# Attention backward on one core: where the X column fills of a row pair stand among its eight units

## The chip, the cores and the metric

One core of one Trainium2 chip runs the whole program. The metric is the device time of one launch in microseconds (us), taken as the median of several runs. Where two kernels are compared, the ratio is the mean time of one kernel's fast runs over that of the other's fast runs of the same rounds, so it isn't quite the ratio of the medians that I quote beside it.

The engines carry their short names: PE multiplies matrices (PEld is its weight load), ACT evaluates functions, DVE and POOL work elementwise, SP issues transfers.

## The reference, cut to what matters

The kernel computes a block of an attention network and all its gradients, for 2 sequences of 4000 tokens and 144 channels.

```python
def _fwd_reference(x, w_qkv, w_att_out, ...):
    xa = _layernorm(x, axis=-1)
    qkv = jnp.einsum('btd,de->bte', xa, w_qkv)
    ...
    scores = jnp.einsum('btd,bsd->bts', q, k) * D ** (-0.5)
    p = _softmax(scores, axis=-1)
    attn = jnp.einsum('bts,bsd->btd', p, v)
    ...                                   # a local branch with convolutions, a merge
def reference(x, ..., grad_out):
    _out, _vjp = jax.vjp(_f, x, ...)
    return (_out, *_vjp(grad_out))
```

## The kernel before

The tokens of a sequence are cut into 32 blocks of 128. The attention stage walks over the 32 row blocks, here called rows `i`. Each row has four *units*, one for every quarter of the columns. Two rows make a *pair* of eight units. I number a pair's units 0 to 7, and units 0 and 4 begin a row.

A unit computes scores `pS` and their gradient counterpart `pD` for 1000 columns, in two halves. A tile `pS`, `pD` or `X` takes one *bank*, a buffer for PE's results; each of the three has two banks. ACT turns `pS` into exponentials `P` (named Pm in the profile), and DVE turns `pD` and `P` into `Sm`:

```python
def unit(i, c2):
    ...
    pS = [ps_s.tile([128, 512], F32, tag="S") for h in range(2)]   # two banks in all
    pD = [ps_d.tile([128, 512], F32, tag="D") for h in range(2)]   # two banks in all
    for r, o_ in enumerate((pS[0], pD[0], pS[1], pD[1])):           # the 16 odd channels, L1768
        nc.tensor.matmul(o_[:, 0:SC], QBr[rr, bi, :], S.XR[rr, c2, 0:SC], start=True, stop=False)
    for w_, p_ in ((QTm, pS), (BTm, pD)):                           # the 128 others, L1772
        for h in range(2):
            nc.tensor.matmul(p_[h][:, 0:SC], w_[:, bi, :], S.xaT[...], start=False, stop=True)
    with tc.high_priority():
        for h in range(2):
            nc.scalar.activation(P[:, pb, c1:c1 + SC], pS[h], ACT.Exp, accum_out=...)
            nc.vector.scalar_tensor_tensor(Sm[:, pb, c1:c1 + SC], pD[h], 1.0, P[...], ..., accum_out=...)
            if c2 == 0 and h == 0 and i > 0:
                row_end2(i - 1)
```

When a row's four units are through, its row sums exist. The *row end* then scales the row's vectors:

```python
def row_end(i):
    nc.vector.reduce_sum(ld[:], ld8[:], axis=AX.X)
    nc.vector.reciprocal(rl[:], ld[:, 0:1])
    ...                                                  # nd, nr and Qs on POOL
    nc.scalar.activation(br[:], S.B_t[:, i, :], ACT.Copy, scale=rl[:])
def row_end2(i):                                          # one unit later, after the first product
    nc.vector.scalar_tensor_tensor(Bt[:, pb, :], Qs[:, pb, :], nd[:], br[:], op0=ALU.mult, op1=ALU.add)
```

The finished row is used twice. `yz` multiplies its transposed blocks by the tokens: 16 matmuls in every unit, for the row two before. After a row's last `yz`, ACT and DVE scale the result `y` (Q_t, yd, B_t in the profile; B_t is that finished result, `Bt` the scaled vector of the newest row). The *X fills* add the row's columns to a running sum `acc`. There are eleven fills for a pair, each of three column blocks with four matmuls a block (the last has two blocks). They run during the next pair:

```python
def xfill(pr, f):
    X = ps_x.tile([128, 3, D], F32, tag="x")              # two banks in all
    for jj in range(nj):
        for kk, i in enumerate((2 * pr, 2 * pr + 1)):
            nc.tensor.matmul(X[:, jj, :], Sm[:, i % NP, ...], Qs[:, i % 4, :], start=(kk == 0), stop=False)
            nc.tensor.matmul(X[:, jj, :], P[:, i % NP, ...], Bt[:, i % 4, :], start=False, stop=(kk == 1))
    ...                                                   # acc += X, on DVE or on ACT and POOL
fills = {(1, 0): 0, (1, 1): 1, (2, 0): 2, (2, 1): 3, (3, 0): 4, (3, 1): 5,
         (4, 0): 6, (4, 1): 7, (5, 1): 8, (6, 0): 9, (6, 1): 10}        # (unit, place): fill
```

In a unit PE runs the score matmuls, then place 0 (a fill, if there is one, and a step of the local branch), the `yz` matmuls, and place 1 (a fill and a step). Units 0 and 7 hold no fill.

Of the kernel before, what the change touches and what calls it, by code (L numbers as in the profile page):

```python
# [8 lines left out]
F32 = mybir.dt.float32  # L9
# [5 lines left out]
D = 144  # L15
# [244 lines left out]
def phase_att(k, W, b, S):  # L260
# [6 lines left out]
    with ExitStack() as es:  # L267
# [149 lines left out]
        def stage_C2(i):  # L417
# [3 lines left out]
            if len(pending) == R_ or i == NB - 1:  # L421
                for j0 in range(0, NB, 3):
                    nj = min(3, NB - j0)
                    X = ps_x.tile([PB, 3, D], F32, tag="x")
                    for jj in range(nj):
                        j = j0 + jj
                        n = len(pending)
                        for kk, (bi_, bpb, bsb) in enumerate(pending):
                            nc.tensor.matmul(X[:, jj, :], Sbuf[0:PB, bsb, j * 128:j * 128 + PB], Qs[:, bpb, :], start=(kk == 0), stop=False)
                            nc.tensor.matmul(X[:, jj, :], Pbuf[0:PB, bpb, j * 128:j * 128 + PB], Bs[:, bpb, :], start=False, stop=(kk == n - 1))  # L430
                    xs = xsp.tile([PB, 3, D], F32, tag="xs")
                    nc.scalar.copy(xs[:, 0:nj, :], X[:, 0:nj, :])
                    nc.gpsimd.tensor_tensor(S.acc[:, j0:j0 + nj, :], xs[:, 0:nj, :], S.acc[:, j0:j0 + nj, :], op=ALU.add)
# [15 lines left out]
def phase_local(k, W, b, S, A):  # L449
# [6 lines left out]
    if True:  # L456
        with ExitStack() as el:
# [185 lines left out]
            def pass3(g):  # L643
# [20 lines left out]
                s1 = sm.tile([PB, GB], F32, tag="s1")  # L664
                nc.vector.reduce_sum(s1[:], dgn[:], axis=AX.X)
                prod = wk.tile([PB, GB, D], F32, tag="prod", bufs=1)
                nc.vector.tensor_tensor(prod[:], dgn[:], gn_tp[:, rsl, :], op=ALU.mult)
                s2 = sm.tile([PB, GB], F32, tag="s2")
                nc.vector.reduce_sum(s2[:], prod[:], axis=AX.X)
                nc1 = sm.tile([PB, GB], F32, tag="nc1")  # L670
# [388 lines left out]
NBK = 32  # L1059
# [659 lines left out]
def phase_attn(k, W, b, S):  # L1719
    nc, tc = k.nc, k.tc  # L1720
    NP = 3
    GW = NBK * 128
    with ExitStack() as es:
# [5 lines left out]
        ps_x = es.enter_context(tc.tile_pool(name="at_psx", bufs=2, space=PSUM))  # L1729
        ps_y = es.enter_context(tc.tile_pool(name="at_psy", bufs=1, space=PSUM))  # L1730
        ps_f = es.enter_context(tc.tile_pool(name="at_psf", bufs=1, space=PSUM))
        P = ab.tile([128, NP, GW], BF, name="Pm")
        Sm = ab.tile([128, NP, GW], BF, name="Sm")
        for t in (P, Sm):
            nc.gpsimd.memset(t[:, :, TT_:], 0.0)
        Qs = ab.tile([128, 4, D], BF, name="Qs")
        Bt = ab.tile([128, 4, D], BF, name="Bt")
        QB = ab.tile([128, 4, 128], BF, name="QB")
        nc.gpsimd.memset(QB[:], 0.0)
        st = {}  # L1740
# [3 lines left out]
        def jit(g):  # L1744
            r = slice(g * 4, g * 4 + 4)
            jt[g] = [xp.tile([128, 4, 128], BF, tag=t_, name=t_) for t_ in ("QTm", "BTm", "QBr")]
            for off, src in ((0, S.Q_t), (32, S.B_t), (64, S.Q_t), (96, S.B_t)):
                nc.gpsimd.tensor_scalar(QB[:, :, off:off + DR], src[:, r, 128:D], 1.0, 0.0, op0=ALU.mult, op1=ALU.add)
            for step in range(3):
                yield 'P', 2  # L1750
                src = (S.Q_t[:, r, 0:128], S.B_t[:, r, 0:128], QB[:])[step]
                pj = ps_f.tile([128, 4, 128], BF, tag="f", name="pj")
                for j in range(4):
                    nc.tensor.transpose(pj[:, j, :], src[:, j, :], id_[:])
                nc.scalar.copy(jt[g][step][:], pj[:])

        def unit(i, c2):
            g, bi = divmod(i, 4)
            QTm, BTm, QBr = jt[g]
            pb = i % NP  # L1760
            if c2 == 0:
                st["ld", i] = sm.tile([128, 2, 8], F32, tag="ld8", name="ld8")
            ld8 = st["ld", i]
            pS = [ps_s.tile([128, 512], F32, tag="S", name="pS") for h in range(2)]
            pD = [ps_d.tile([128, 512], F32, tag="D", name="pD") for h in range(2)]
            for r, o_ in enumerate((pS[0], pD[0], pS[1], pD[1])):
                rr = slice(32 * r, 32 * r + DR)
                nc.tensor.matmul(o_[:, 0:SC], QBr[rr, bi, :], S.XR[rr, c2, 0:SC], start=True, stop=False)  # L1768
            c0 = 2 * c2 * SC
            for w_, p_ in ((QTm, pS), (BTm, pD)):  # L1770
                for h in range(2):
                    nc.tensor.matmul(p_[h][:, 0:SC], w_[:, bi, :], S.xaT[:, c0 + h * SC:c0 + (h + 1) * SC], start=False, stop=True)  # L1772
            with tc.high_priority():
                for h in range(2):
                    c1 = c0 + h * SC
                    n = 2 * c2 + h
                    nc.scalar.activation(P[:, pb, c1:c1 + SC], pS[h][:, 0:SC], ACT.Exp, accum_out=ld8[:, 0, n:n + 1])  # L1777
                    nc.vector.scalar_tensor_tensor(Sm[:, pb, c1:c1 + SC], pD[h][:, 0:SC], 1.0, P[:, pb, c1:c1 + SC], op0=ALU.mult, op1=ALU.mult,  # L1778
                                                   accum_out=ld8[:, 1, n:n + 1])
                    if c2 == 0 and h == 0 and i > 0:  # L1780
                        row_end2(i - 1)

        def flip(key, i, h):

            t = st[key, i, h] = ab.tile([128, 16, 128], BF, tag=key, bufs=3, name=key)
            nc.sync.dma_start_transpose(out=t[:], in_=(P if key == "PT" else Sm)[:, i % NP, h * 2048:(h + 1) * 2048])
# [17 lines left out]
        def row_end2(i):  # L1804
            pb = i % 4
            nc.vector.scalar_tensor_tensor(Bt[:, pb, :], Qs[:, pb, :], st.pop(("nd", i))[:], st.pop(("br", i))[:], op0=ALU.mult, op1=ALU.add)  # L1806
# [16 lines left out]
                nc.scalar.activation(yd[:], y[:, 0, :], ACT.Copy, scale=nr[:])  # L1823
                nc.vector.scalar_tensor_tensor(S.Zn[:, i, :], y[:, 1, :], rl[:], yd[:], op0=ALU.mult, op1=ALU.add)  # L1824

        def xfill(pr, f):
            j0 = f * 3
            nj = min(3, NBK - j0)
            X = ps_x.tile([128, 3, D], F32, tag="x", name="X")
            for jj in range(nj):  # L1830
                j = j0 + jj
                for kk, i in enumerate((2 * pr, 2 * pr + 1)):
                    nc.tensor.matmul(X[:, jj, :], Sm[:, i % NP, j * 128:(j + 1) * 128], Qs[:, i % 4, :], start=(kk == 0), stop=False)  # L1833
                    nc.tensor.matmul(X[:, jj, :], P[:, i % NP, j * 128:(j + 1) * 128], Bt[:, i % 4, :], start=False, stop=(kk == 1))  # L1834
            a_ = S.acc[:, j0:j0 + nj, :]
            if f % 2 == 1:
                xs = xp.tile([128, 3, D], F32, tag="xs", name="xs")
                nc.scalar.copy(xs[:, 0:nj, :], X[:, 0:nj, :])  # L1838
                nc.gpsimd.tensor_tensor(a_, xs[:, 0:nj, :], a_, op=ALU.add)  # L1839
            else:  # L1840
                nc.vector.tensor_tensor(a_, X[:, 0:nj, :], a_, op=ALU.add)  # L1841



        fills = {(1, 0): 0, (1, 1): 1, (2, 0): 2, (2, 1): 3, (3, 0): 4, (3, 1): 5, (4, 0): 6, (4, 1): 7, (5, 1): 8, (6, 0): 9, (6, 1): 10}
        Q = Steps()
        local_steps(k, W, b, S, es, ps_f, Q)
        with tc.manual_schedule():
            for _ in jit(0):
                pass  # L1850
            for g in range(1, NGR):
                Q.add(32 * g - 16, jit(g))
            for i in range(NBK + 2):
                pr, half = i // 2 - 1, i % 2
                for c2 in range(4):
                    if i < NBK:
                        unit(i, c2)
                    if c2 == 0 and i == NBK:
                        row_end2(i - 1)
                    for place in range(2):  # L1860
                        f = fills.get((half * 4 + c2, place))
                        if f is not None and 0 <= pr < NBK // 2:
                            xfill(pr, f)
                        Q.place()
                        if place == 0 and 0 <= i - 2 < NBK:
                            yz(i - 2, c2)
                        if place == 0:
                            key, fi, h = (("PT", i - 1, 1), (None, 0, 0), ("PT", i, 0), ("ST", i, 0))[c2]
                            if key and 0 <= fi < NBK:
                                flip(key, fi, h)  # L1870
                            if c2 == 2 and 0 <= i - 1 < NBK:
                                flip("ST", i - 1, 1)
                    if c2 == 3 and i < NBK:
                        row_end(i)
            while Q.tasks:
                Q.place()
# [442 lines left out]
```

## Time and profile before

| | before |
|---|---|
| time, median of 3 runs | 1528.79 us (1527.81 to 1530.97) |
| span of the profiled run | 1533.1 us |
| attention, first unit to last, both sequences | 1039.5 us |
| one pair, mean from the fifth row on | 32.8 us at full clock (33.25 us with the parts at half clock) |

The first line of the profile page gives busy time, share of the span and instruction count for each engine.

```profile
PE 1364.5 (89%) x15366; PEld 990.8 (65%) x15366; DVE 886.1 (58%) x3021; ACT 820.7 (54%) x2473; POOL 567.4 (37%) x1049
```

PE looks nearly full, but the Trainium skill warns of this line (Perfetto Trace Analysis, "Identifying the Most-Contended Engine"): matmul busy time isn't a good measure of how close PE is to its limit, because matmuls are pipelined. The next two lines are groups of that page. Their columns are line, engine, operation, tiles, shapes and count, then busy us and mean ns of one, then idle us of the engine just before them and what ended it.

```profile
L1834 PE MATMUL X<-Bt,Pm 128*128 128x144 bf16 x2048 | 293.6, 227 | 1.0 <-DVE Bt L1806 1.0
...
L1768 PE MATMUL pD<-XR,QBr 16*128 16x500 bf16 x512 | 131.0, 392 | 21.1 <-DVE Sm L1778 19.6
```

One X matmul "takes" 227 ns. Yet in the timeline they start every 62 ns, so three or four are always in flight, and an idle engine shows as idle only after the last of them has drained. I therefore read stalls from start to start. The following lines are timelines of PE, ACT and DVE for the passage from unit 7 to unit 1 of one pair. The columns are start us, us, engine, line, operation, tiles, shapes and count, with the idle time before it and its releaser in brackets.

```profile
303.00 0.38 PE L1768 MATMUL pD<-XR,QBr 16*128 16x500 bf16 x1
...
305.29 1.16 PE L1816 MATMUL y<-xaa,PT 128*128 128x144 bf16 x16
...
306.63 0.38 PE L1768 MATMUL pD<-XR,QBr 16*128 16x500 bf16 x1
...
307.17 0.37 PE L1768 MATMUL pD<-XR,QBr 16*128 16x500 bf16 x1 [0.15 <-DVE Sm L1778]
307.47 0.60 PE L1772 MATMUL pS<-xaT,QTm 128*128 128x500 bf16 x2
...
303.18 0.38 ACT L1821 ACTIVATE Q_t<-y,rl 128x144 bf16<-128x144 f32 x1
303.44 0.39 ACT L1823 ACTIVATE yd<-y,nr 128x144 f32<-128x144 f32 x1
304.54 0.42 ACT L1801 ACTIVATE br<-B_t,rl 128x144 f32<-128x144 bf16 x1 [0.71 <-DVE rl L1794]
304.86 0.57 ACT L1777 ACTIVATE Pm<-pS 128x500 bf16<-128x500 f32 x1
...
303.86 0.37 DVE L1824 SCALAR_TENSOR_TENSOR B_t<-y,rl,yd 128x144 bf16<-128x144 f32 x1 [0.40 <-ACT yd L1823]
304.15 0.16 DVE L1792 TENSOR_REDUCE ld<-ld 128x2 f32<-128x16 f32 x1
304.34 0.16 DVE L1794 RECIPROCAL rl<-ld 128x1 f32<-128x1 f32 x1
305.55 0.68 DVE L1778 SCALAR_TENSOR_TENSOR Sm<-pD,Pm 128x500 bf16<-128x500 f32 x1 [1.05 <-ACT Pm L1777]
...
306.15 0.36 DVE L1806 SCALAR_TENSOR_TENSOR Bt<-Qs,nd,br 128x144 bf16<-128x144 bf16 x1
306.43 0.67 DVE L1778 SCALAR_TENSOR_TENSOR Sm<-pD,Pm 128x500 bf16<-128x500 f32 x1
```

Unit 0 starts at 303.00 and unit 1 at 306.63. In unit 1 the last of the four L1768 matmuls should start some 10 ns after the first; it starts 0.54 us later, because DVE's second product of unit 0 has only then left its `pD` bank. The profile calls 0.15 us of this idle.

The other lines show why the product is late. ACT scales the `y` of unit 7 (303.18 and 303.44), and DVE makes B_t of it. Only then does DVE reach the row sum and its reciprocal (304.15, 304.34). ACT's `br` waits for that reciprocal, and unit 0's exponentials stand behind `br` (304.86). The products (305.55, 306.43) and `Bt` (306.15) follow. I call this the *row-end chain*.

### The profile page before, as it was taken

How to read it: one execution, taken by the hardware profiler on the slowest of the kernel's cores; microseconds unless marked ns; L12 is line 12 of the kernel's file. 1: busy time of each engine (PE TensorE's matmuls, PEld its weight loads, DVE VectorE, ACT ScalarE, POOL GpSimd, SP SyncE). 2: the span in 40 equal slices, each digit the busy share in tenths (PEclk: the TensorE clock that was granted, in tenths of full speed). 3: DMA queues.
4: the chain of work that ended last, by engine and by line, in shares of the span. 5: the costliest groups of instructions: out<-in, count | busy, mean ns of one | idle time of the engine just before them, and what ended most of it. 6: DMA issues, size and time to landing. Idle time of an engine off the chain costs nothing. (4 is left out here: it accounts for less than half of the span.)

```text
span 1533.1 us, 40191 instructions
## 1 busy us (share of the span) xinstructions
PE 1364.5 (89%) x15366; PEld 990.8 (65%) x15366; DVE 886.1 (58%) x3021; ACT 820.7 (54%) x2473; POOL 567.4 (37%) x1049
## 2 busy tenths in 40 slices
PE   5989999999999999899779999999999999989932
PEld 3727767676776767687553767677667667868610
DVE  5545676676676666344335666676776676534332
ACT  4746656566656654343365666666656565444210
POOL 2233444444344433343232444344444442334200
PEclk9959999999999999999896999999999999999955
DMA  5348978898988799654525988998999988856320
GB/s 143 105 86 149 169 136 162 155 170 150 163 153 163 131 192 171 146 171 116 158 77 99 165 153 147 170 164 154 164 160 147 170 158 163 162 156 180 78 87 13
DMA packets 652289, 220.66 MB, mean 144 GB/s; under 512 B 589876, under 2 KB 649012, under 8 KB 652084
## 3 DMA queue, kind: packets, MB, share of 16 engines
q1 hardware_dynamic: 651220, 217.89, 73.0%
q8 instruction: 122, 2.00, 0.6%
q14 instruction: 83, 0.68, 0.2%
q10 hardware_dynamic: 864, 0.09, 0.0%
HBM read 58.00 MB, written 25.13 MB: 54 GB/s over the span
## 5 line engine op out<-in xcount | busy, mean ns | idle before, releaser
L1778 DVE SCALAR_TENSOR_TENSOR Sm<-pD,Pm 128x500 bf16<-128x500 f32 x512 | 331.2, 675 | 286.8 <-ACT Pm L1777 226.4
L1777 ACT ACTIVATE Pm<-pS 128x500 bf16<-128x500 f32 x512 | 294.9, 582 | 125.9 <-PE pS L1772 123.0
L1839 POOL TENSOR_TENSOR acc<-xs,acc 128x432 f32<-128x432 f32 x160 | 179.8, 1124 | 395.9 <-ACT xs L1838 393.9
L1834 PE MATMUL X<-Bt,Pm 128*128 128x144 bf16 x2048 | 293.6, 227 | 1.0 <-DVE Bt L1806 1.0
L1833 PE MATMUL X<-Qs,Sm 128*128 128x144 bf16 x2048 | 293.7, 227 | 0.5 <-POOL Qs L1797 0.5
L1833 PEld LDWEIGHTS <-Sm 128*128 128x128 bf16 x2048 | 201.5, 98 | 19.2 <-issue 2.6
L1834 PEld LDWEIGHTS <-Pm 128*128 128x128 bf16 x2048 | 201.2, 98 | 18.8 <-issue 2.1
L1772 PE MATMUL pS<-xaT,QTm 128*128 128x500 bf16 x512 | 162.0, 400 | 0.0
L1772 PE MATMUL pD<-xaT,BTm 128*128 128x500 bf16 x512 | 160.1, 396 | 0.0
L1838 ACT COPY xs<-X 128x432 f32<-128x432 f32 x160 | 83.2, 520 | 138.4 <-PE X L1834 137.4
L1816 PE MATMUL y<-xaa,PT 128*128 128x144 bf16 x2048 | 150.4, 227 | 1.2 <-DVE B_t L1824 1.2
L1768 PE MATMUL pD<-XR,QBr 16*128 16x500 bf16 x512 | 131.0, 392 | 21.1 <-DVE Sm L1778 19.6
L1816 PE MATMUL y<-xaa,ST 128*128 128x144 bf16 x2048 | 149.0, 226 | 0.0
L1816 PEld LDWEIGHTS <-PT 128*128 128x128 bf16 x2048 | 134.1, 98 | 9.2 <-issue 1.6
L1816 PEld LDWEIGHTS <-ST 128*128 128x128 bf16 x2048 | 131.9, 98 | 6.5
L1841 DVE TENSOR_TENSOR acc<-X,acc 128x432 f32<-128x432 f32 x192 | 111.1, 578 | 42.3 <-PE X L1834 42.3
L1768 PE MATMUL pS<-XR,QBr 16*128 16x500 bf16 x512 | 117.3, 395 | 5.4 <-ACT Pm L1777 4.1
L1777 ACT ACTIVATION_READ_ACCUMULATOR Pm<-pS 128x1 f32 x512 | 102.2, 200 | 0.0
L1772 PEld LDWEIGHTS <-QTm 128*128 128x128 bf16 x512 | 29.3, 98 | 106.6 <-issue 106.6
L1772 PEld LDWEIGHTS <-BTm 128*128 128x128 bf16 x512 | 52.4, 102 | 65.3 <-issue 11.4
L2009 POOL TENSOR_SCALAR cc<-xaa,n 128x144 f32<-128x144 bf16 x64 | 36.2, 572 | 99.3 <-DVE n L2006 84.1
L1768 PEld LDWEIGHTS <-QBr 16*128 16x128 bf16 x1024 | 30.3, 91 | 61.7 <-issue 36.7
(584 smaller groups left out, 2602.6 us busy)
## 6 DMA issues: line engine op xcount, KB each, us to landing
gs<-in_grad_out_dram SPq DMA_DIRECT2D x24, 720.0 KB
gtap<-gn_d SPq DMA_DIRECT2D x16, 720.0 KB
dh_d<-dh SPq DMA_DIRECT2D x32, 144.0 KB
dhr<-dh_d SPq DMA_DIRECT2D x16, 288.0 KB
gs<-in_grad_out_dram SPq DMA_DIRECT2D x8, 540.0 KB
xg<-in_x_dram SPq DMA_DIRECT2D x28, 144.0 KB
dug_d<-dug SPq DMA_DIRECT2D x16, 144.0 KB
gn_d<-gn_t SPq DMA_DIRECT2D x32, 72.0 KB
```

What stands on the lines that cost most here:

```text
L1768: nc.tensor.matmul(o_[:, 0:SC], QBr[rr, bi, :], S.XR[rr, c2, 0:SC], start=True, stop=False)
L1772: nc.tensor.matmul(p_[h][:, 0:SC], w_[:, bi, :], S.xaT[:, c0 + h * SC:c0 + (h + 1) * SC], start=False, stop=True)
L1777: nc.scalar.activation(P[:, pb, c1:c1 + SC], pS[h][:, 0:SC], ACT.Exp, accum_out=ld8[:, 0, n:n + 1])
L1778: nc.vector.scalar_tensor_tensor(Sm[:, pb, c1:c1 + SC], pD[h][:, 0:SC], 1.0, P[:, pb, c1:c1 + SC], op0=ALU.mult, op1=ALU.mult, accum_out=l ...
L1816: nc.tensor.matmul(y[:, w, :], src[:, jj, :], S.xaa[:, j, :], start=(j == 0), stop=(j == NBK - 1))
L1833: nc.tensor.matmul(X[:, jj, :], Sm[:, i % NP, j * 128:(j + 1) * 128], Qs[:, i % 4, :], start=(kk == 0), stop=False)
L1834: nc.tensor.matmul(X[:, jj, :], P[:, i % NP, j * 128:(j + 1) * 128], Bt[:, i % 4, :], start=False, stop=(kk == 1))
L1838: nc.scalar.copy(xs[:, 0:nj, :], X[:, 0:nj, :])
L1839: nc.gpsimd.tensor_tensor(a_, xs[:, 0:nj, :], a_, op=ALU.add)
L1841: nc.vector.tensor_tensor(a_, X[:, 0:nj, :], a_, op=ALU.add)
L2009: nc.gpsimd.tensor_scalar(cc[:, q, :], S.xaa[:, 2 * p + q, :], n[:, 1, q:q + 1], n[:, 0, q:q + 1], op0=ALU.mult, op1=ALU.add)
```

## The change

The change leaves no unit without a fill. Fills 0 and 1 are split by row. The half of the pair's first row runs in unit 7, before the pair's own turn. The half of its second row runs in unit 0. The other nine fills move along.

```diff
-        def xfill(pr, f):
+        def xfill(pr, f, rows=(0, 1)):
-            X = ps_x.tile([128, 3, D], F32, tag="x", name="X")
-            for jj in range(nj):
-                j = j0 + jj
-                for kk, i in enumerate((2 * pr, 2 * pr + 1)):
-                    nc.tensor.matmul(... Sm ... Qs ..., start=(kk == 0), stop=False)
-                    nc.tensor.matmul(... P ... Bt ..., start=False, stop=(kk == 1))
+            if 0 in rows:
+                st["X", f] = ps_x.tile([128, 3, D], F32, tag="x", name="X")
+            X = st["X", f]
+            for kk in rows:
+                i = 2 * pr + kk
+                for jj in range(nj):
+                    j = j0 + jj
+                    nc.tensor.matmul(... Sm ... Qs ..., start=(kk == 0 and jj == 0), stop=False, skip_group_check=True)
+                    nc.tensor.matmul(... P ... Bt ..., start=False, stop=(kk == 1), skip_group_check=True)
+            if 1 not in rows:
+                return
 ...
-        fills = {(1, 0): 0, (1, 1): 1, (2, 0): 2, ...}                    # as above
+        fills = {(0, 1): ((0, (1,)), (1, (1,))), (1, 0): ((2, (0, 1)),), (1, 1): ((3, (0, 1)),), (2, 1): ((4, (0, 1)),),
+                 (3, 0): ((5, (0, 1)),), (3, 1): ((6, (0, 1)),), (4, 1): ((7, (0, 1)),), (5, 0): ((8, (0, 1)),),
+                 (5, 1): ((9, (0, 1)),), (6, 1): ((10, (0, 1)),), (7, 1): ((0, (0,)), (1, (0,)))}
```

A half-finished fill holds three column blocks open in one PSUM bank, which is why the start flag now stands on the first matmul of the bank alone. The Trainium skill (PSUM — Partial Sum Buffer, "The four PSUM rules") says that a starting matmul clears the accumulation bits of the whole bank, and that groups which are open at once in a bank may have the flag on the first matmul issued there alone. The changed kernel follows that rule. Whole fills now also run row by row instead of block by block.

More of the change, by code (lines that the diff above doesn't have):

```diff
@@ L1824, in yz @@
                 nc.vector.scalar_tensor_tensor(S.Zn[:, i, :], y[:, 1, :], rl[:], yd[:], op0=ALU.mult, op1=ALU.add)
-        def xfill(pr, f):
+        def xfill(pr, f, rows=(0, 1)):
             j0 = f * 3
             nj = min(3, NBK - j0)
-            X = ps_x.tile([128, 3, D], F32, tag="x", name="X")
-            for jj in range(nj):
-                j = j0 + jj
-                for kk, i in enumerate((2 * pr, 2 * pr + 1)):
-                    nc.tensor.matmul(X[:, jj, :], Sm[:, i % NP, j * 128:(j + 1) * 128], Qs[:, i % 4, :], start=(kk == 0), stop=False)
-                    nc.tensor.matmul(X[:, jj, :], P[:, i % NP, j * 128:(j + 1) * 128], Bt[:, i % 4, :], start=False, stop=(kk == 1))
+            if 0 in rows:
[5 more added lines that the diff above has]
+                    j = j0 + jj
+                    nc.tensor.matmul(X[:, jj, :], Sm[:, i % NP, j * 128:(j + 1) * 128], Qs[:, i % 4, :], start=(kk == 0 and jj == 0), stop=False, skip_group_check=True)
+                    nc.tensor.matmul(X[:, jj, :], P[:, i % NP, j * 128:(j + 1) * 128], Bt[:, i % 4, :], start=False, stop=(kk == 1), skip_group_check=True)
+            if 1 not in rows:
+                return
+            st.pop(("X", f))
             a_ = S.acc[:, j0:j0 + nj, :]
@@ L1841, in xfill @@
                 nc.vector.tensor_tensor(a_, X[:, 0:nj, :], a_, op=ALU.add)
-        fills = {(1, 0): 0, (1, 1): 1, (2, 0): 2, (2, 1): 3, (3, 0): 4, (3, 1): 5, (4, 0): 6, (4, 1): 7, (5, 1): 8, (6, 0): 9, (6, 1): 10}
+        fills = {(0, 1): ((0, (1,)), (1, (1,))), (1, 0): ((2, (0, 1)),), (1, 1): ((3, (0, 1)),), (2, 1): ((4, (0, 1)),), (3, 0): ((5, (0, 1)),), (3, 1): ((6, (0, 1)),),
+                 (4, 1): ((7, (0, 1)),), (5, 0): ((8, (0, 1)),), (5, 1): ((9, (0, 1)),), (6, 1): ((10, (0, 1)),), (7, 1): ((0, (0,)), (1, (0,)))}
         Q = Steps()
@@ L1860, in phase_attn @@
                     for place in range(2):
-                        f = fills.get((half * 4 + c2, place))
-                        if f is not None and 0 <= pr < NBK // 2:
-                            xfill(pr, f)
+                        for f, rows in fills.get((half * 4 + c2, place), ()):
+                            q = pr + 1 if rows == (0,) else pr
+                            if 0 <= q < NBK // 2:
+                                xfill(q, f, rows)
                         Q.place()
```

## The prediction

> **What bounds the kernel.** Page, part 1: PE busy 1364.5 of 1533.1 us (89%), DVE 58%, ACT 54%. The chain that ended last is mostly PE. The attention stage (timeline, about 83 to 620 and 803 to 1340 us) is bound by PE's in-order stream. PE's busy share hides stalls there, because matmuls overlap, so I read start-to-start gaps in the timeline. TensorE: Matmul & The Clock Gate (the Trainium skill, "Back-to-back issue gap") gives N/2.4 + 2.5 ns, 62.5 ns at N=144; the timeline agrees (X and y matmuls start 62 ns apart). Per row pair (eight units) PE takes 33.1 us, of which about 29.2 us is pace (my sum) and 3.9 us stall.
>
> Where the stalls are, at full clock, ns per unit (PE work / stall at the next unit's head):
> - unit 0: 2502 / 1125, plus 500 inside
> - unit 7: 2560 / 195
> - unit 4: 3945 / 350; unit 5: 3349 / 300
> - units 1, 2, 3, 6 (work 3.8 us and over): about none.
>
> Cause: units 0 and 7 hold no X fills, so PE reaches the next unit's 16-row score matmuls before ACT's exponentials (0.58 us each) and DVE's products (0.67 us) have freed pS and pD. In unit 0 they are late because ACT and DVE first run row-end work after unit 7's y: scaled copies of y, reciprocal, br, then the exponential.
>
> **What the change does.** No arithmetic is added or removed: same 4096 X matmuls and evacuations. 12 X matmuls (0.75 us) move into each of units 0 and 7, one more fill into unit 5; units 2, 4 and 6 lose a fill each. New: fills 0 and 1 hold both X buffers from unit 7 to unit 0, and unit 0's halves need Bt of the row just ended. In the trace Bt ends 3.8 us after unit 0's start, 0.9 us after y ends. So PE will wait for Bt inside unit 0, but less: unit 7's y, where the row-end chain begins, now ends 0.75 us earlier relative to unit 0's start. I expect Bt about 3.0 us after it and a wait of 0.3 us.
>
> **Sum per pair (estimate from these lengths),** head stalls counted with the unit that caused them: units 7+0 7.4 us before, 7.3 after though 1.5 us of work moved in; unit 1 unchanged; unit 2 -0.6; unit 4 -0.25 (0.75 less work, but its row-end chain then shows as about 1 us of stall at unit 5's head); unit 5 +0.45; unit 6 -0.55. Net -1.1 us of 33.1, all on the critical path. Some 30 of 32 pairs: -33 us, discounted to -29 because waits move and ps_f (one buffer) stays. Head and tail stages do not change.
>
> **Prediction:** 1500 us, range 1481 to 1520. Faster by over 2%: 0.46; within 2%: 0.51; slower by over 2%: 0.03.
>
> **What would show it.** The stall at unit 1's head (0.96 us start to start, the pD score matmul waiting for DVE's Sm) falls under 0.3; the X<-Bt group shows a new wait for Bt in unit 0, under 0.5 us each; unit 5's head stall grows; PE busy falls by about 25 us at equal counts; DVE, ACT and POOL busy stay within 1%.
>
> **What would make it wrong.** Bt may come no earlier, if local work on ACT rather than y's end sets it: then some 16 us are saved. Unit 4's chain, with fill 6's DVE sum now ahead of the row sum, may lose more than 0.5 us. Or the even spread also removes ps_f stalls, and over 40 us are saved. The half-clock spells (3.4 us each, a few in attention) may shift either way.

## The result, and the profile after

| | before | after |
|---|---|---|
| median | 1528.93 us (4 runs) | 1510.10 us (4 runs, 1509.91 to 1512.44) |
| ratio | | 0.9871, 95% interval 0.9847 to 0.9894 |
| span of the profiled run | 1533.1 us | 1510.5 us |
| attention, first unit to last, both sequences | 1039.5 us | 1008.5 us |
| drains, last unit's start to last X matmul, both | 39.0 us | 42.5 us |
| from the first drain to the second attention stage | 179.4 us | 181.2 us |
| from the second drain to the end | 192.1 us | 195.6 us |

The change saves 18.8 us, and the ratio says 1.3%. The outputs are right. The same line of the page, and the same two groups, for the changed kernel:

```profile
PE 1351.8 (89%) x15366; PEld 991.2 (66%) x15366; DVE 875.8 (58%) x3021; ACT 815.9 (54%) x2473; POOL 566.1 (37%) x1049
```

```profile
L1837 PE MATMUL X<-Bt,Pm 128*128 128x144 bf16 x2048 | 292.2, 226 | 15.6 <-DVE Bt L1806 15.5
...
L1768 PE MATMUL pD<-XR,QBr 16*128 16x500 bf16 x512 | 121.3, 390 | 10.8 <-DVE Sm L1778 10.4
```

The idle time before the `pD` matmuls fell from 21.1 to 10.8 us, and a new wait stands before the X matmuls that need `Bt`: 15.6 us instead of 1.0. The timelines of PE, ACT and DVE for unit 0 of one pair of the changed kernel show it. DVE's lines begin with the last product of unit 7.

```profile
328.16 0.38 PE L1768 MATMUL pS<-XR,QBr 16*128 16x500 bf16 x1
...
330.34 0.23 PE L1836 MATMUL X<-Qs,Sm 128*128 128x144 bf16 x1
331.51 0.22 PE L1837 MATMUL X<-Bt,Pm 128*128 128x144 bf16 x1 [0.94 <-DVE Bt L1806]
...
332.61 0.38 PE L1768 MATMUL pS<-XR,QBr 16*128 16x500 bf16 x1
...
329.48 0.41 ACT L1801 ACTIVATE br<-B_t,rl 128x144 f32<-128x144 bf16 x1 [0.84 <-DVE rl L1794]
329.80 0.57 ACT L1777 ACTIVATE Pm<-pS 128x500 bf16<-128x500 f32 x1
...
326.47 0.67 DVE L1778 SCALAR_TENSOR_TENSOR Sm<-pD,Pm 128x500 bf16<-128x500 f32 x1
...
328.09 0.37 DVE L1824 SCALAR_TENSOR_TENSOR B_t<-y,rl,yd 128x144 bf16<-128x144 f32 x1 [0.16 <-ACT yd L1823]
328.38 0.30 DVE L1604 TENSOR_SCALAR a__5755<-a__5755 128x576 bf16<-128x576 bf16 x1
328.71 0.46 DVE L1605 TENSOR_TENSOR h_t<-a__5755,hs 128x576 bf16<-128x576 bf16 x1
329.08 0.16 DVE L1792 TENSOR_REDUCE ld<-ld 128x2 f32<-128x16 f32 x1
329.28 0.17 DVE L1794 RECIPROCAL rl<-ld 128x1 f32<-128x1 f32 x1
330.49 0.68 DVE L1778 SCALAR_TENSOR_TENSOR Sm<-pD,Pm 128x500 bf16<-128x500 f32 x1 [1.04 <-ACT Pm L1777]
...
331.09 0.36 DVE L1806 SCALAR_TENSOR_TENSOR Bt<-Qs,nd,br 128x144 bf16<-128x144 bf16 x1
331.38 0.67 DVE L1778 SCALAR_TENSOR_TENSOR Sm<-pD,Pm 128x500 bf16<-128x500 f32 x1
```

Unit 0 starts at 328.16. Its first X matmul runs at 330.34, and the second waits 1.17 us for `Bt`, which DVE finishes at 331.45. On DVE the row's last product started at 326.47, but B_t and two operations of the local branch (L1604, L1605) stand in the queue ahead of the row sum (329.08). `br` waits for the reciprocal, and the exponentials wait behind `br`. Unit 1 then starts with no stall at all (332.61): the wait for `Bt` has taken the place of the wait for the bank.

The next table gives mean lengths in us of the eight units at full clock, from the fifth row on (23 to 28 units each; a unit with any half-clock time in it is left out). A stall at a unit's head is counted with the unit before it, which causes it. The pair is taken from start to start of its units, so it can differ from the sum of the rows by 0.1 us.

| unit | before | after | difference | predicted difference |
|---|---|---|---|---|
| 7 and 0 together | 7.33 | 7.82 | +0.49 | -0.1 |
| 1 | 4.06 | 4.15 | +0.09 | 0 |
| 2 | 4.35 | 3.64 | -0.71 | -0.6 |
| 3 | 4.38 | 4.38 | 0 | 0 |
| 4 | 4.70 | 4.44 | -0.26 | -0.25 |
| 5 | 4.08 | 4.47 | +0.39 | +0.45 |
| 6 | 3.98 | 3.41 | -0.57 | -0.55 |
| pair | 32.82 | 32.23 | -0.59 | -1.1 |

With their half-clock parts the pairs took 33.25 us before and 32.23 us after, 1.02 us less: five half-clock spells (stretches of the clock record at 0.5, 3.41 us each) lie in these pairs in the trace of the kernel before, and none in that of the changed kernel.

Three mean stalls a pair matter for the argument. The one at unit 1's head went from 0.96 us to none, the one at unit 5's head from 0.33 to 0.66 us, and the wait for `Bt` inside unit 0 from none to 0.69 us.

Outside these stretches the changed kernel's profiled run lost 8.8 us: 3.5 us in the drains and 5.3 us in the stages after them, whose code is the same. The next lines give busy us (and count) of PE, PEld, DVE, ACT and POOL in the two stretches that follow the drains, then the granted PE clock, the DMA share and GB/s. First the kernel before, then the changed one:

```profile
623.60:803.10 179.50, 149.87 (x1693) 118.53 (x1690) 68.97 (x282) 76.58 (x221) 61.27 (x119) 0.92 0.47 136
1341.00:1533.10 192.10, 129.39 (x1398) 92.08 (x1395) 68.49 (x286) 50.53 (x158) 42.77 (x84) 0.80 0.37 103
```

```profile
608.30:789.50 181.20, 151.64 (x1692) 119.98 (x1689) 68.84 (x282) 76.56 (x221) 61.09 (x119) 0.91 0.46 135
1314.90:1510.50 195.60, 135.65 (x1399) 96.70 (x1396) 68.47 (x286) 50.51 (x158) 42.67 (x84) 0.76 0.36 101
```

All five engines do the same work in both. The clock differs: 0.80 against 0.76 in the last stretch. In the trace's clock record the half-clock time of the two stretches is 27.2 and 78.0 us before, 33.8 and 92.7 us after.

### The profile page after: what moved, and what is told of

It reads as the page before. It is cut to its first block, busy times and chain, and to the rows that moved or that the text cites. A ratio compares the mean times of both kernels' runs of the same rounds, so it can differ in the third digit from the quotient of the medians.

```text
span 1510.5 us, 40195 instructions
## 1 busy us (share of the span) xinstructions
PE 1351.8 (89%) x15366; PEld 991.2 (66%) x15366; DVE 875.8 (58%) x3021; ACT 815.9 (54%) x2473; POOL 566.1 (37%) x1049
## 5 line engine op out<-in xcount | busy, mean ns | idle before, releaser
L1777 ACT ACTIVATE Pm<-pS 128x500 bf16<-128x500 f32 x512 | 294.5, 581 | 89.8 <-PE pS L1772 86.8
L1837 PE MATMUL X<-Bt,Pm 128*128 128x144 bf16 x2048 | 292.2, 226 | 15.6 <-DVE Bt L1806 15.5
L1772 PE MATMUL pD<-xaT,BTm 128*128 128x500 bf16 x512 | 156.9, 389 | 0.0
L1816 PEld LDWEIGHTS <-PT 128*128 128x128 bf16 x2048 | 132.8, 98 | 11.5 <-issue 2.6
L1816 PEld LDWEIGHTS <-ST 128*128 128x128 bf16 x2048 | 132.6, 98 | 11.6
L1768 PE MATMUL pD<-XR,QBr 16*128 16x500 bf16 x512 | 121.3, 390 | 10.8 <-DVE Sm L1778 10.4
L1768 PE MATMUL pS<-XR,QBr 16*128 16x500 bf16 x512 | 111.7, 393 | 1.7 <-ACT QBr L1755 1.4
```

The costliest lines, as they stand in the source:

```text
L1772: nc.tensor.matmul(p_[h][:, 0:SC], w_[:, bi, :], S.xaT[:, c0 + h * SC:c0 + (h + 1) * SC], start=False, stop=True)
L1777: nc.scalar.activation(P[:, pb, c1:c1 + SC], pS[h][:, 0:SC], ACT.Exp, accum_out=ld8[:, 0, n:n + 1])
L1816: nc.tensor.matmul(y[:, w, :], src[:, jj, :], S.xaa[:, j, :], start=(j == 0), stop=(j == NBK - 1))
L1837: nc.tensor.matmul(X[:, jj, :], P[:, i % NP, j * 128:(j + 1) * 128], Bt[:, i % 4, :], start=False, stop=(kk == 1), skip_group_check=True)
```

## The experiments

Eleven runs beside the changed kernel's own. Runs of one heading ran on one chip and are compared with each other. The changed kernel itself wasn't run in the first call; there its 1510.10 us comes from its own run, in which the kernel before took 1528.93 us against 1529.90 us in the first call.

### First call: four runs around the row-end chain

**bt_stale.** Unit 0's halves use a row that is long ready. Its output is wrong, which doesn't matter for the time.

```diff
-   nc.tensor.matmul(X[:, jj, :], P[...], Bt[:, i % 4, :], ...)
+   nc.tensor.matmul(X[:, jj, :], P[...], Bt[:, (i - 1 if rows == (1,) else i) % 4, :], ...)
```

> Changed kernel, but unit 0's half fills multiply by the scaled row (Bt) of the row before, which is ready long ago, so that PE has no wait for Bt there; the result is wrong on purpose, the work is the same. Changed kernel: 1510.1 us, mean wait for Bt in unit 0 0.69 us per pair, head stall of unit 1 zero. Theory (one row-end chain holds both Bt and, 0.67 us later, the free pD bank): the wait moves to the pD score matmul at unit 1's head, about 0.4 us of it comes back there, and at most 0.3 us per pair is saved: 1499 to 1507 us. Rival (the split made a new wait that is pure loss): all 0.69 us per pair comes back, about 21 us: 1486 to 1492 us.

Measured: 1495.29 us, between the two ranges. The trace shows what the edit itself did. The wait for `Bt` (0.69 us) was gone, 0.29 us came back at unit 1's head, and a pair took 32.03 us instead of 32.23. The other 0.2 us came back elsewhere in units 0 to 2 and isn't traced further. The attention stages took 1003.2 us, 5.3 us less than in the changed kernel's trace. The rest of the 15 us lies in stages that the edit doesn't touch, where half-clock time was 19.7 and 80.8 us. So the theory's mechanism and its limit of 0.3 us a pair hold for the attention stage, though less came back at unit 1's head than the 0.4 us expected, and the total was blurred; stale_g80 below repeats it.

**seven_front.** Unit 7's halves stand ahead of its `yz` matmuls.

```diff
-   (7, 1): ((0, (0,)), (1, (0,)))}
+   (7, 0): ((0, (0,)), (1, (0,)))}
```

> Changed kernel, but unit 7's 12 X matmuls stand before its y matmuls rather than after them. The count of matmuls in each unit is the same. Theory (the row-end chain starts at the end of unit 7's y, and the X matmuls after y buy it 0.75 us): Bt comes later after unit 0's start, about 3.7 us instead of 3.2, the wait for Bt rises from 0.69 to about 1.2 us per pair, 1520 to 1528 us. Rival (only how many matmuls a unit holds counts, not their place): 1507 to 1513 us.

Measured: 1523.72 us. `Bt` ended 3.62 us after unit 0's start (3.22 in the changed kernel), and the wait for it was 0.91 us. Matmul counts per unit are the same, so place counts and not only number. The wait rose less than expected, by 0.22 us rather than 0.5. Unit 0 itself grew from 4.28 to 4.69 us.

**after_sum** and **before_sum.** The row sum and its reciprocal are issued straight after the row's last product, on the changed kernel and on the kernel before.

```diff
     with tc.high_priority():
         for h in range(2):
             ...                                    # exponentials and products
+        if c2 == 3:
+            row_sum(i)                             # reduce_sum and reciprocal, taken out of row_end
```

> Changed kernel, with the row sum and its reciprocal issued on DVE straight after the row's last product rather than behind the local work and the y scaling that follow. Theory (the row-end chain sets what is left): Bt 2.3 to 2.7 us after unit 0's start instead of 3.2, wait for Bt under 0.2 us instead of 0.69, head stall of unit 5 under 0.25 us instead of 0.66; 0.8 to 1.1 us per pair saved, 1476 to 1486 us. Rival (ACT and DVE throughput sets it, whatever the order): less than 5 us saved, 1505 us and over.

Measured: 1474.15 us, ratio to the kernel before 0.9638 (0.9608 to 0.9669). The wait for `Bt` fell from 0.69 to 0.26 us a pair, unit 5's head stall from 0.66 to 0.10 us, and a pair took 31.05 us, 1.18 us less. The gain and the time lie just beyond the expected ranges, and `Bt` (2.8 us after unit 0's start in the mean) and its wait just short of theirs. These timelines of PE, ACT and DVE show the same unit 0 as above, which now starts at 322.53:

```profile
322.53 0.38 PE L1768 MATMUL pS<-XR,QBr 16*128 16x500 bf16 x1
...
324.71 0.23 PE L1842 MATMUL X<-Qs,Sm 128*128 128x144 bf16 x1
325.01 0.22 PE L1843 MATMUL X<-Bt,Pm 128*128 128x144 bf16 x1
...
322.90 0.42 ACT L1807 ACTIVATE br<-B_t,rl 128x144 f32<-128x144 bf16 x1
...
320.84 0.67 DVE L1778 SCALAR_TENSOR_TENSOR Sm<-pD,Pm 128x500 bf16<-128x500 f32 x1
...
321.55 0.17 DVE L1793 TENSOR_REDUCE ld<-ld 128x2 f32<-128x16 f32 x1
321.76 0.17 DVE L1795 RECIPROCAL rl<-ld 128x1 f32<-128x1 f32 x1
...
322.61 0.36 DVE L1830 SCALAR_TENSOR_TENSOR B_t<-y,rl,yd 128x144 bf16<-128x144 f32 x1
...
324.59 0.37 DVE L1812 SCALAR_TENSOR_TENSOR Bt<-Qs,nd,br 128x144 bf16<-128x144 bf16 x1
```

The row sum now follows the product at once (321.55), `br` waits for nothing, and the first exponential starts 0.74 us after unit 0's start instead of 1.64 us. `Bt` ends 2.43 us after the start instead of 3.29 us.

> The kernel before, with the same early row sum and nothing else. Theory: what the spread hid is mostly this chain, so the early sum alone brings about as much as the change: head stall of unit 1 0.96 to about 0.3 us, of unit 5 0.33 to under 0.1, 1498 to 1510 us. Rival (units 0 and 7 are too short whatever the chain: two exponentials and two products take 2.5 us): under 8 us saved, 1521 us and over.

Measured: 1488.58 us, ratio 0.9740 (0.9704 to 0.9776). I had expected about the change's own gain, and it was twice that: the early sum alone saves 41 us where the change saves 19 us. A pair took 31.68 us. Unit 1's head stall fell only to 0.64 us, which fits the rival's point that units without fills are too short; with the spread on top (after_sum) it is gone, and the time falls by another 14 us. So over the whole pair the late sum cost more than the empty units did. The two don't act at the same place, though: of the 1.14 us that the early sum saves in a pair at full clock, 0.7 us lies in units 4 and 5 (4.70 to 4.24 us and 4.08 to 3.82 us), at the row end in the middle of the pair, where unit 4 keeps a fill in both kernels.

### Second call: the parts, and the stages after

**after_again.** The changed kernel once more, as a control.

> The changed kernel again, unchanged, beside the three others on one chip: 1506 to 1513 us. It is the control for how far the half-clock spells after the attention stages differ between executions of one kernel: in the first trace of this kernel they were 30.7 us between the stages and 20.5 us after the second (without the last one of 74 us), and in the other traces so far each further us of spell went with about 0.5 us of tail. If the spells belong to the kernel, they come back within 3.4 us; if they are luck of the moment, they differ by more.

Measured: 1511.65 us (1506.39 to 1514.94). Attention 1011.2 us and drains 42.5 us came back. Half-clock time after the first drain was 26.3 us, not 33.8, and that stretch took 177.4 us, not 181.2. After the second drain it was 89.8 us (92.7 in the first trace). So part of it is luck of the moment and part comes back.

**after_g80.** In the stage after attention, one POOL copy moves ahead of two that wait for a load.

```diff
 def prep(g):
+    nc.gpsimd.tensor_scalar(g80[...], G["gs", g][:, :, :, 128:D], 1.0, 0.0, ...)
     nc.gpsimd.tensor_scalar(t3[:, r, 0:32], dh[:, r, 256:2 * D], 1.0, 0.0, ...)
     nc.gpsimd.tensor_scalar(t3[:, r, 32:48], S.Zn[:, r, 128:D], 1.0, 0.0, ...)
-    nc.gpsimd.tensor_scalar(g80[...], G["gs", g][:, :, :, 128:D], 1.0, 0.0, ...)
```

> Changed kernel, with one POOL copy (g80) of the stage after attention issued ahead of two that wait for a load, so that PE's 2.25 us wait for it at the handover shrinks. Theory (that idle time at the handover is what trips the half clock there): both the idle time and part of the spells go, the two tails shorten together by 6 to 12 us, 1498 to 1505 us. Rival (the spells come from elsewhere, or the next wait, for the load of ug, takes its place): 0 to 4 us, 1506 to 1511 us.

Measured: 1500.09 us, 11.6 us less than the control. Two timelines of PE at the first handover, the changed kernel and then this one, show the wait that went:

```profile
610.66 0.22 PE L1950 MATMUL EF<-Q_t,gs 128*128 128x144 bf16 x1 [1.13 <-DVE B_t L1824]
...
613.70 0.34 PE L1950 MATMUL EF<-Q_t,g 128*80 128x144 bf16 x1 [2.25 <-POOL g L1923]
```

```profile
610.81 0.22 PE L1950 MATMUL EF<-Q_t,gs 128*128 128x144 bf16 x1 [1.12 <-DVE B_t L1824]
...
611.43 0.23 PE L1950 MATMUL EF<-Q_t,g 128*80 128x144 bf16 x1
```

PE waited 1.13 us for B_t and then 2.25 us for the copy, and only the first wait is left. The two stretches after the drains (columns as before) ran at a higher clock, and with 13.3 and 82.4 us of half-clock time:

```profile
608.80:780.10 171.30, 143.90 (x1687) 114.00 (x1684) 68.74 (x282) 76.48 (x221) 60.58 (x119) 0.96 0.49 143
1306.70:1497.40 190.70, 130.70 (x1399) 92.67 (x1396) 68.44 (x286) 50.45 (x158) 42.55 (x84) 0.78 0.37 103
```

They took 362.0 us against 372.7 us of the control, 10.7 us less. Two waits of about 2.25 us account for 4.5 us; the rest came with 20.4 us less half-clock time. That the wait trips the half clock is not shown by this: before_g80 below speaks against it.

**split_only.** Fills 0 and 1 are split as in the change; all others stay where the kernel before has them, so unit 1 has none.

```diff
-   fills = {(1, 0): 0, (1, 1): 1, (2, 0): 2, ...}
+   fills = {(0, 1): halves of row 1, (2, 0): 2, ..., (6, 1): 10, (7, 1): halves of row 0}
```

> Only the split part of the change: fills 0 and 1 by halves in units 7 and 0, all other fills where the kernel before has them, so that unit 1 holds none. Per-unit lengths from the traces: units 7 and 0 +0.53 us, unit 1 from 4.32 to about 3.0 us, the others as before: 32.3 us a pair at full clock, 1506 to 1516 us. So the theory says that the split carries the change and that moving fills 4 to 10 as well brings under 5 us. Rival (the even spread is what pays, and an empty unit 1 stalls as unit 0 did): unit 2's head stall over 0.8 us, 1520 us and over.

Measured: 1513.13 us, ratio 0.9894 (0.9849 to 0.9938); the change beside it 0.9866. A pair took 32.40 us at full clock. Unit 1 fell from 4.06 to 3.17 us although unit 2's head now stalls by 0.49 us: an empty unit that no row end follows costs less than unit 0 did. The split carries the change. Moving the other fills brings the control 0.10 us a pair more (32.30 us) and loses 4.7 us in the drains (37.8 to 42.5 us). Most of that loss is one stall: in each sequence the last unit's head waits 1.30 us in the changed kernel and not at all here or in the kernel before. Attention is 9 us shorter in the control's trace (1020.1 to 1011.2 us), but 5 us of that lies in two pairs in which the split_only trace has a half-clock spell and the control's has none.

**best.** All three repairs on the changed kernel: the early row sum, the `g80` copy first, and in all fills the `Qs` matmuls ahead of those that need `Bt` (over both halves in unit 0).

> Changed kernel with the early row sum, the six Qs matmuls of unit 0's halves ahead of the six that need Bt, and the g80 copy first. With the early sum alone 1474.2 us, wait for Bt 0.26 us per pair. Theory: that wait falls to under 0.05 us, of which half is kept (0.1 us per pair, 4 us), and the handover brings 0 to 8 us: 1463 to 1472 us. Rival (nothing left there, other waits take over): 1472 us and over.

Measured: 1462.42 us (1459.64 to 1467.30) and correct, ratio 0.9560 (0.9521 to 0.9600). The wait for `Bt` fell to 0.06 us, and a pair took 30.84 us. It beats both kernels.

### Third call: the change with the handover repaired on both sides

This chip was slower: the kernel before took 1538.80 us beside these runs.

**after_g80_again.** The edit of after_g80, as a control.

> The changed kernel with the g80 copy first, again, as the control of the next two on one chip: 1497 to 1505 us. Between the stages its half-clock spells should again be under 20 us.

Measured: 1503.47 us. Half-clock time after the first drain was 24.9 us, not under 20: the spells came back in part.

**before_g80.** The same edit on the kernel before.

> The kernel before with the g80 copy first: the change measured with the handover repaired on both sides. Theory (part of what the change earned in the attention stages was given back in drains and in half-clock spells of the stages after them, about 5 us of spells): the repair is worth less here than the 11.5 us it brought the changed kernel, 5 to 8 us, so 1521 to 1526 us, and the change is worth 21 to 26 us between the two repaired kernels. Rival (the spells have no part in it): the repair is worth 11.5 us here too, 1517 to 1520 us, and the change 17 to 20 us.

Measured: 1534.14 us, 4.7 us under the kernel before (ratio 0.9963). The same repair brought the changed kernel 11.6 us, in another call. Between the repaired kernels the change is worth 30.7 us (1534.14 to 1503.47). The absolute range was missed because the chip was slower. The repair's 4.7 us is just under the theory's 5 to 8, and the change's 30.7 us is above its 21 to 26; the rival's 11.5 and 17 to 20 us are further off. Repaired or not, the attention stages of the kernel before took 1039.5 us. In this trace the 2.25 us waits are gone too, yet the half-clock time after the drains was 28.4 and 87.0 us, not less than the 27.2 and 78.0 us without the repair. So the theory's figures fit better, but what trips the half clock in those stages stays open.

**stale_g80.** The edits of bt_stale and after_g80 together.

> The kernel with the ready row in unit 0's halves (wrong on purpose) with the g80 copy first, against the first run of this call: what the wait for Bt costs, without the spells that blurred the first measurement (1495 us, of which the trace put 5 to 8 us into the attention stages and about 10 us into stages that the edit does not touch). Theory: 5 to 9 us less than the control of this call. Rival (the wait is pure loss): 18 us less or more.

Measured: 1502.84 us, 0.6 us less than the control, against 5 to 9 expected. In the trace the attention stages took 5.4 us less and the drains 1.3 us less, as the theory has it; the two stretches after them took 3.2 us more, with 3.3 and 1.9 us more half-clock time. So 1495 us was no measure of the wait. That the wait is pure loss is refuted; that removing it saves the 5 us that attention shows is seen in two traces but not in this total.

## Why the prediction was right

The time lay inside the range, and the class within 2% had the largest chance, if barely (0.51 against 0.46 for faster). Of the forecast 29 us, 18.8 came. The mechanism was right, but a pair at full clock saved only 0.59 of the forecast 1.1 us; the shortfall is one term of its sum, units 7 and 0 (+0.49 us, not -0.1). That the total still came to 18.8 us owes something to luck in the forecast: half-clock spells, of which the prediction said only that they may shift either way, left the attention stage. Point by point:

- **Stalls in units 0 and 7 hide in PE's busy share, and fills there absorb them: right.** Unit 1's head stall went from 0.96 us to none, and split_only shows that this part carries the gain.
- **The wait for Bt: right in kind, mis-sized.** "I expect Bt about 3.0 us after it and a wait of 0.3 us"; measured 3.22 us and 0.69 us. Units 7 and 0 were put at 7.3 us and took 7.82. The reason is in the prediction's own list of what could go wrong: local work also holds the row sum back, on DVE rather than on ACT. after_sum shows it, since moving the sum alone took 0.43 us off the wait.
- **The wait isn't the whole loss.** Taking it away (bt_stale) gave 0.20 us a pair and not 0.69, because the bank for unit 1 becomes free only when DVE has finished the product behind `Bt` (0.29 us); the other 0.2 us that came back is not traced.
- **Units 2, 4, 5 and 6: right,** within 0.12 us each. Unit 5's head stall doubled, though to 0.66 us and not "about 1 us".
- **"Head and tail stages do not change": wrong.** Attention as a whole saved 28 to 31 us, near the forecast for the pairs. The drains took back 3.5 us, of which 2.6 us is the stall of the last unit's head, where the local work has run out and the unit before it holds only 8 X matmuls. The stages after took 1 to 5 us more, with more half-clock time. The two sums, from the two traces of the changed kernel against the one of the kernel before: 31.0 - 3.5 - 5.3 = 22.2 us, and 28.3 - 3.5 - 1.2 = 23.6 us, less 1.2 us in the head stage (before the first unit, 83.0 and 84.2 us). The spans differ by 22.6 and 22.5 us. The step from there to 18.8 us is scatter: the profiled execution of the kernel before, with its span of 1533.1 us, was slower than each of its timed runs (1530.97 us at most).
- **Attention got help that I had not counted.** Inside it the half-clock time fell from 78.6 to 55.4 us. At 0.59 us each, 32 pairs would make 19 us of its 31.0 us (an estimate); the other 12 us I put down to the clock, by subtraction. It wasn't a chance of one execution: the repaired kernel before had 77.9 us, and three more traces of the changed kernel, two of them repaired, 55.7 to 57.6 us.
- **PE's busy time** fell by 12.7 us and not 25 (the page counts overlapping matmuls, and slow ones longer). ACT and POOL stayed within 1%; DVE fell by 1.2%.

It stays open why the half-clock time after attention differs between executions of one kernel (33.8 and 26.3 us, or 13.3 and 24.9 us).

## What to carry to other kernels

Before you spread work to fill an engine's gaps, follow the late result back through each engine's queue of work. Here a two-instruction sum stood behind work that could be done later, and moving it saved twice what spreading the work saved; the two together saved more than either. Judge a local change by its own stage in the trace, since stages that an edit didn't touch moved by up to 12 us here (bt_stale, 365.2 us after the drains, against 376.8 us).

## What the Trainium skill lacked or had wrong

- TensorE: Matmul & The Clock Gate, "Why this matters for your kernels", asks for no PE idle gap over about 3 us. (Its "A second HAM failure mode: psum-queue depth-cycling" does tell of short idle times that made the clock swing, but gives no length.) Here shorter gaps came before half-clock spells. These lines of the PE timeline of the kernel before show unit 0 and the head of unit 1:

```profile
272.22 0.37 PE L1768 MATMUL pS<-XR,QBr 16*128 16x500 bf16 x1 [1.11 <-ACT Pm L1777]
272.94 0.37 PE L1768 MATMUL pD<-XR,QBr 16*128 16x500 bf16 x1 [0.35 <-DVE Sm L1778]
...
273.82 0.37 PE L1768 MATMUL pD<-XR,QBr 16*128 16x500 bf16 x1 [0.49 <-DVE Sm L1778]
274.12 1.01 PE L1772 MATMUL pS<-xaT,QTm 128*128 128x500 bf16 x2
```

  The reported gaps are 1.11, 0.35 and 0.49 us, together 1.95 us within 2.7 us. At 274.1 the clock record shows half clock for 3.41 us, and two 500-column matmuls then take 1.01 us instead of 0.60. The kernel before has five such spells inside its steady attention, each in a unit 0 or at the head of the unit 1 behind it; the changed kernel has none.
- The same page, "What's actually happening", gives two clock states and a window of 3413 ns. The traces agree: every spell runs at 0.5 and lasts 3.41 us or a multiple of it, but for the last of a trace. The page's "Terms" puts the cost of half-clock time at half of it, and doesn't say whether that holds for a stage that also waits for other engines. Here it was a little less: between 19.6 us of it (split_only, 175.3 us) and 33.8 us (the changed kernel, 181.2 us) the stretch after the first drain grew by 0.42 us for each further us.
- The same page, "Back-to-back issue gap": the formula that it calls the isolated one (62.5 ns for 144 columns) is what streams of weight loads and matmuls show here, 62 ns from start to start. The 81 ns that it gives for such streams at 128 columns isn't seen: those of L1504, each with its weight load, start 56 ns apart.
- The page says that the slow start of a kernel varies between runs. That the whole time of one kernel on one chip may scatter with its granted clock, no page says: seven runs of the kernel before in the first call took 1526.11 to 1535.80 us at clocks of 0.943 to 0.935.
